# Retention followed by a convolution-gated unit: half of the convolution moved from TensorE to three other engines in every second unit

## The chip, the cores and the metric

The kernel runs on one core of one Trainium2 chip. The metric is the device time of one execution in microseconds (us), as the median of several. A core has five engines that matter here: TensorE (PE in the profile; PEld is its weight load), VectorE (DVE), ScalarE (ACT), GpSimd (POOL) and SyncE (SP), which only starts transfers. Each works through its own list of instructions in order and waits for the others through semaphores.

## What is computed

Two layers, one after the other. The first is a causal linear attention ("retention"), in which the score of two tokens decays with their distance. The second gates a projection of the result with the sigmoid of a causal convolution over five tokens, one weight per channel and tap.

```python
scores = scale * np.matmul(q, k.transpose(0, 1, 3, 2))       # (8, 8, 576, 576), head size 64
Dmat = np.where(rel >= 0, gamma[:, None, None] ** rel, 0.0)  # rel = row - column
x = np.matmul(scores * Dmat, v)                              # then heads joined: (8, 576, 512)
for k in range(5):
    gate_pre += conv_w[k] * xp[:, k:k + S, :]                # xp: x with four zero rows in front
gate = 1.0 / (1.0 + np.exp(-gate_pre))
out = (gate * (x @ w_val)) @ w_out                           # (8, 576, 512), float32
```

Products are taken in bfloat16 and summed in float32.

## The kernel before

**Tiles.** The 576 tokens of a batch are four whole chunks of 128 and a tail of 64; two tails of two batches share a chunk. That makes 36 chunks: four batches' whole chunks (0 to 15), their tails (16, 17), and the same for the other four batches (18 to 35). The first layer works chunk by chunk, the second on units of two chunks, so unit n is chunks 2n and 2n+1, and there are 18. In the second layer channels lie on partitions, in four blocks of 128.

**First layer, for a chunk t.** GpSimd starts the load of the keys (`load_keys`), scales and casts the values (`cast_v`) and casts the queries (`cast_q`). `turn_k` and `turn_q` transpose keys and queries on TensorE, four matmuls each, into a PSUM tile `tps`, of which there is one (`ps_t`, one buffer), and a copy takes it to SBUF: for keys on VectorE (kt), for queries on ScalarE (qtb, or qt for a tail). `scores` multiplies them into two PSUM banks, `masks(t, 0)` and `masks(t, 1)` apply the causal mask on VectorE (p). `carried` and `values` sum the chunk's output o from the running state and from p, and `take_x` scales it on VectorE into `xg`, which holds x for four batches with four zero columns ahead of each. `update` adds the chunk to the state in PSUM, `take_state` copies it out with two ScalarE instructions (sbd, or sbl at a batch's end).

**Second layer, for a unit n.** `conv` does the convolution as matmuls with diagonal weights `dg`: 64 x 64 tiles, four of which use different quarters of the array; five taps, four blocks, so 40 matmuls of 256 columns into two banks. In each half-block the order is such that a bank holds half of one block and half of another, and the value weights `wvb` and the output weights `wob` have their channels in the same mixed order. `gate` takes the sigmoid of a bank on ScalarE, `value` multiplies x with `wvb` (eight matmuls for each of two halves) and VectorE multiplies the gate into it (z). `project` multiplies z with `wob`, 128 tokens at a time, ScalarE copies the result (ob), SyncE stores it. The banks of conv, value and project come from one ring of three (`ps_g`).

**Order.** Nothing is planned by a scheduler: the program order is written out by hand, a head for chunks 0 to 3 and then a loop over t from 4 to 37, whose passes are called steps here. Step t does the state and output of chunk t, the scores of chunk t+1, `turn_k` of chunk t+2, the cast of v for t+2, the load of keys for t+4, and one or two `turn_q` for later batches (in steps 5 to 28, 32 and 33). An even step also does conv, gates and values of unit n = t/2 - 1, an odd step the projection of that unit:

```python
            n = t // 2 - 1
            ...
            if unit and not odd and n > 1:
                conv(n)
                gate(n, 0)
                gate(n, 1)
            if ok(t + 2) and t > 4:
                turn_k(t + 2)
            if ok(t) and odd:
                take_x(t)
            if ok(t + 1) and odd:
                masks(t + 1, 1)
            part = project if odd else value
```

So in an odd step VectorE's list is p, kt, x, p, and in an even one p, x, p, kt, z, z. In both, `turn_q` stands on TensorE between the two halves of `value` or `project`.

## Time and profile before

The median of three runs is 170.65 us (170.41 to 170.76). The profiled execution spans 169.9 us.

| what | us | instructions |
|---|---|---|
| conv's matmuls, line 385 | 23.2 busy | 720 |
| value's matmuls, line 400 | 36.9 busy | 288 |
| project's matmuls, line 411 | 36.5 busy | 144 |
| masks on VectorE, line 289 (128 x 512) | 0.686 each | 62 of the main form |
| take_x on VectorE, line 331 | 0.681 each | 31 |
| kt's copy on VectorE, line 249 | 0.423 each | 33 |
| gate on ScalarE, line 393 | 0.594 each | 36 |
| ob's copy on ScalarE, line 414 | 0.586 each | 36 |
| half of a state's copy on ScalarE, line 363 | 0.367 each | 64 |
| cast_v on GpSimd, line 221 | 1.049 each | 35 |
| start of a key load on GpSimd, line 96 | 0.941 each | 30 |

Busy time is the time in which an engine worked on at least one instruction of a group; matmuls overlap, so 720 of 271 ns give 23.2 us. A bracket at the end of a timeline line says how long the engine was idle before it and on whom it waited. The TensorE clock was granted in full over the whole span. 16 DMA engines moved 35.23 MB at 207 GB/s on average.

### The profile page before, as it was taken

The numbers are of one execution on the slowest core, as the hardware profiler recorded it, in microseconds if no ns is written. First come the engines' busy times: TensorE is split into PE (matmuls) and PEld (weight loads), VectorE is DVE, ScalarE is ACT, GpSimd is POOL, SyncE is SP. The second block draws the span as 40 slices with busy tenths as digits, with TensorE's granted clock in tenths as the row PEclk, the third lists the DMA queues.
The fourth block names the chain that finished last, engine by engine and source line by source line (L and its number), as shares of the span: only waits on it lengthen the run. The fifth ranks groups of instructions, "written<-read, shape, count | busy, mean of one in ns | idle before, by whom it ended". The sixth has DMA issues, their size and how long they took to land.

```text
span 169.9 us, 5543 instructions
## 1 busy us (share of the span) xinstructions
PE 154.0 (91%) x2297; PEld 110.4 (65%) x2297; DVE 114.3 (67%) x218; ACT 90.6 (53%) x184; POOL 97.9 (58%) x130
## 2 busy tenths in 40 slices
PE   6768874889999999999999999999999999999970
PEld 1344643645868686868677776868686867778630
DVE  6676670477676777777777768777777788786330
ACT  6754433736657556565437465755656543644330
POOL 8559999059279978487279338827986463000000
PEclk9999999999999999999999999999999999999999
DMA  4999999999999999999999999999999992303214
GB/s 124 291 198 275 319 198 270 193 185 169 287 296 275 252 235 221 129 237 280 272 198 171 281 258 183 202 289 276 253 267 190 190 230 92 124 3 127 83 44 123
DMA packets 93958, 35.23 MB, mean 207 GB/s; under 512 B 80090, under 2 KB 88814, under 8 KB 93934
## 3 DMA queue, kind: packets, MB, share of 16 engines
q1 hardware_dynamic: 57744, 29.63, 66.5%
q0 software_dynamic: 36000, 4.98, 43.0%
q8 instruction: 18, 0.29, 0.7%
q10 hardware_dynamic: 190, 0.27, 0.6%
q14 instruction: 6, 0.05, 0.1%
HBM read 30.42 MB, written 9.44 MB: 235 GB/s over the span
## 4 chain that ended last, share of the span: by engine, by line
PE 75%; DMA 9%; SPq 5%; DVE 3%; ACT 2%; issue 2%; POOL 1%; ACTq 0%; DVEq 0%
PE g L400 17%; PE g L411 16%; PE g L385 12%; PE tps L241 10%; PE s L280 6%; PE o L321 6%; DMA kb<-in_k_dram 5%; DMA fvc<-in_v_dram 4%; SPq L78 4%; PE st L352 3%; PE o L304 2%; SPq L119 1%; DVE p L289 1%; ACT ob L414 1%; ACT qtb L263 1%
## 5 line engine op out<-in xcount | busy, mean ns | idle before, releaser
L289 DVE TENSOR_TENSOR p<-s,maskq 128x512 bf16<-128x512 f32 x62 | 42.2, 686 | 16.6 <-PE s L280 16.4
L221 POOL TENSOR_TENSOR vb<-fvc,gin 128x512 bf16<-128x512 f32 x35 | 36.7, 1049 | 23.6 <-DMA fvc<-in_v_dram 7.5
L403 DVE TENSOR_TENSOR z<-gate,g 128x512 bf16<-128x512 f32 x36 | 24.8, 688 | 24.9 <-PE g L400 18.2
L400 PE MATMUL g<-xg,wvb 128*128 128x256 bf16 x288 | 36.9, 273 | 0.0
L411 PE MATMUL g<-wob,z 128*128 128x512 bf16 x144 | 36.5, 379 | 0.3 <-DVE z L403 0.3
L414 ACT COPY ob<-g 128x512 f32<-128x512 f32 x36 | 21.1, 586 | 27.7 <-PE g L411 27.4
L393 ACT ACTIVATE gate<-g 128x512 f32<-128x512 f32 x36 | 19.5, 594 | 20.8 <-PE g L385 20.8
L400 PEld LDWEIGHTS <-wvb 128*128 128x128 bf16 x288 | 26.5, 98 | 3.5 <-issue 0.8
L96 POOL DMA_DIRECT2D kb<-in_k_dram x30 | 28.2, 941 | 0.3 <-issue 0.2
L234 POOL CAST qb<-fqb 128x512 bf16<-128x512 f32 x27 | 16.6, 621 | 14.8 <-DMA fqb<-in_q_dram 14.8
L385 PE MATMUL g<-xg,dg 64*64 64x256 bf16 x720 | 23.2, 271 | 0.0
L363 ACT CAST sbd<-st 64x256 bf16<-64x256 f32 x48 | 17.6, 367 | 8.9 <-PE st L352 8.4
L331 DVE TENSOR_TENSOR xg<-o,gout 128x512 bf16<-128x512 f32 x31 | 21.1, 681 | 1.0 <-PE o L321 1.0
L385 PEld LDWEIGHTS <-dg 64*64 64x64 bf16 x720 | 18.4, 106 | 2.3 <-issue 0.8
L411 PEld LDWEIGHTS <-z 128*128 128x128 bf16 x144 | 12.5, 98 | 10.5 <-DVE z L403 1.2
L241 PE MATMUL tps<-ident,kb 128*128 128x128 bf16 x144 | 14.5, 224 | 2.6 <-DMA kb<-in_k_dram 1.7
L263 ACT COPY qtb<-tps 128x512 bf16<-128x512 bf16 x24 | 14.1, 589 | 4.2 <-PE tps L241 4.2
L280 PE MATMUL s<-qtb,kt 64*128 64x128 bf16 x248 | 12.3, 219 | 2.9 <-DVE kt L249 1.4
L249 DVE COPY kt<-tps 128x512 bf16<-128x512 bf16 x33 | 14.0, 423 | 0.9 <-PE tps L241 0.7
L321 PE MATMUL o<-p,vb 128*64 128x128 bf16 x280 | 14.5, 225 | 0.0
L241 PEld LDWEIGHTS <-qb 128*128 128x128 bf16 x144 | 10.9, 99 | 5.2 <-ACT qb L234 0.7
L241 PEld LDWEIGHTS <-kb 128*128 128x128 bf16 x144 | 8.5, 98 | 8.5 <-issue 2.8
(72 smaller groups left out, 147.0 us busy)
## 6 DMA issues: line engine op xcount, KB each, us to landing
fqb<-in_q_dram SPq DMA_DIRECT2D x8, 1024.0 KB, 9.2
fvc<-in_v_dram SPq DMA_DIRECT2D x32, 256.0 KB, 8.8
out_dram<-ob SPq DMA_DIRECT2D x32, 256.0 KB, 5.1
kb<-in_k_dram POOLq DMA_DIRECT2D x30, 128.0 KB, 8.4
wvf<-in_moe_w_val_dram SPq DMA_DIRECT2D x1, 1024.0 KB, 7.3
fqc<-in_q_dram SPq DMA_DIRECT2D x8, 128.0 KB, 5.9
fvc<-in_v_dram SPq DMA_DIRECT2D x8, 128.0 KB, 5.1
out_dram<-ob SPq DMA_DIRECT2D x6, 128.0 KB, 3.2
```

The lines of the kernel that those rows point to most:

```text
L96: nc.gpsimd.dma_start(out=kb, in_=k[b, :, c * P:(c + 1) * P, :].rearrange("h p d -> p h d"))
L221: eng.tensor_tensor(vb, loaded["v", *chunks[t]], gin[:, chunks[t][2], :].unsqueeze(2).to_broadcast([P, H, D]), op=ALU.mult)
L241: nc.tensor.transpose(ps[:, pr, :], flat[:, pr * P:(pr + 1) * P], ident)
L280: nc.tensor.matmul(s[i][:, pr, :], lhsT=kt[r, pr, :], rhs=queries(t, r, pr), start=(pr == 0), stop=(pr == NP - 1), skip_group_check=True)
L289: nc.vector.tensor_tensor(p, sps[t][i], m.unsqueeze(1).to_broadcast([P, NP, P]), op=ALU.mult)
L321: nc.tensor.matmul(o[r, pr, :], lhsT=vb[:, 2 * pr + i, :], rhs=pt[t, i][:, pr, :], start=(fresh and pr == 0), stop=(pr == NP - 1), skip_gr ...
L331: nc.vector.tensor_tensor(by_token(x[:, bl, :, PAD + i0:PAD + i0 + P]), ops[t].rearrange("p o (r n) -> p o n r", r=RQ), by_token(gout[:, : ...
L385: nc.tensor.matmul(g[bank][cols, pr, :], lhsT=dg[rows, blk, kk, :], rhs=xs(n, rows, blk, kk), start=(pr == 0 and kk == 0), stop=(pr == 1 a ...
L400: nc.tensor.matmul(vps[:, j, :], lhsT=wvb[:, o, 2 * i + j, :], rhs=xs(n, slice(0, P), o, PAD), start=(j == 0 and o == 0), stop=(j == 1 and ...
L403: nc.vector.tensor_tensor(z, gsb[n][i], vps, op=ALU.mult)
L411: nc.tensor.matmul(o, lhsT=zsb[n, j // 2][:, j % 2, i * P:(i + 1) * P], rhs=wob[:, j, :], start=(j == 0), stop=(j == NP - 1))
L414: nc.scalar.copy(ob, o)
```

## The change

In units 2, 4, ..., 16 (`aside`) the convolution of blocks 2 and 3 is no longer done by TensorE. Block 2 is summed on VectorE: one multiplication and four multiply-adds of 128 x 256 into a float32 tile `acc0`. Block 3 is done on ScalarE and GpSimd: ScalarE multiplies x by the tap's weight (an `Identity` activation with a scale per partition) and GpSimd adds the products into `acc1`. The sigmoid then takes two instructions a bank, one from PSUM and one from the sum in SBUF. As these blocks lie in natural order, such units use `wvn` and `won`, copies of the weights' second half in that order.

To give the taps time, everything of a unit comes one step later: conv, gates and values of unit n in step 2n+3 (in step 36 for the last), its projection in step 2n+4 (37 for the last). The taps are spread: the first one or two in step 2n+1, two more in 2n+2, the rest at the start of 2n+3. `take_x` and the second mask come ahead of `turn_k` in every step now. In the steps 2n+2 and 2n+3 of such a unit kt is copied on ScalarE instead of VectorE. Step 6 has no work of the second layer any more; step 36 has the projection of unit 16, and then conv and values of unit 17. The purpose is to take work off TensorE.

```diff
+        aside = set(range(2, NT // 2, 2))
+        def tap(eng, n, i, kk):
...
+            if i == 1:
+                t = a
+                if kk:
+                    t = gp.tile([P, 2 * P], F32, name="tap")
...
+                nc.scalar.activation(t, x, AF.Identity, scale=w)
+                if kk:
+                    nc.gpsimd.tensor_tensor(a, a, t, op=ALU.add)
+            elif kk == 0:
+                eng.tensor_scalar(a, x, w, None, op0=ALU.mult)
+            else:
+                eng.scalar_tensor_tensor(a, in0=x, scalar=w, in1=a, op0=ALU.mult, op1=ALU.add)
...
-            for pr in range(2):
+            for pr in range(1 if n in aside else 2):
...
+            if n in aside:
+                nc.scalar.activation(t[:, 0, :], gps[n][i][:, 0, :], AF.Sigmoid)
+                nc.scalar.activation(t[:, 1, :], acc[n, i], AF.Sigmoid)
...
+            first = next((n for n in range(2, NT // 2) if t == min(2 * n + 3, NT)), None)
+            second = 0 if t == 4 else 1 if t == 5 else next((n for n in range(2, NT // 2) if t == min(2 * n + 4, NT + 1)), None)
+            on_act = any(t in (2 * n + 2, 2 * n + 3) for n in aside)
...
+            for n in aside:
+                if t == 2 * n + 3:
+                    tap(None, n, 1, 4)
+                    tap(nc.vector, n, 0, 3)
+                    tap(nc.vector, n, 0, 4)
...
                 values(t)
-                if not odd:
-                    take_x(t)
-            if ok(t + 1) and not odd:
+                take_x(t)
+            if ok(t + 1):
                 masks(t + 1, 1)
-            if unit and not odd and n > 1:
-                conv(n)
-                gate(n, 0)
-                gate(n, 1)
+            if first is not None and t < NT:
+                conv(first)
+                gate(first, 0)
+                gate(first, 1)
             if ok(t + 2) and t > 4:
-                turn_k(t + 2)
-            if ok(t) and odd:
-                take_x(t)
-            if ok(t + 1) and odd:
-                masks(t + 1, 1)
+                turn_k(t + 2, s_copy if on_act else v_copy)
+            for n in aside:
+                if t == 2 * n + 1:
+                    tap(None, n, 1, 0)
+                    tap(None, n, 1, 1)
+                    tap(nc.vector, n, 0, 0)
+                if t == 2 * n + 2:
+                    tap(None, n, 1, 2)
+                    tap(None, n, 1, 3)
+                    tap(nc.vector, n, 0, 1)
+                    tap(nc.vector, n, 0, 2)
+            part, n = (value, first) if first is not None and t < NT else (project, second)
...
+            if t == NT:
+                conv(first)
+                for i in range(2):
+                    gate(first, i)
+                for i in range(2):
+                    value(first, i)
```

## The prediction

> **What bounds the kernel now.** I read the page's busy shares first, then its forty slices, then the costliest groups (the conv's, line 385, had no idle time before it), and last the timelines of two steps in the middle of the run, where the order on each engine can be seen. From the page:

> ```profile
> PE 154.0 (91%) x2297; PEld 110.4 (65%) x2297; DVE 114.3 (67%) x218; ACT 90.6 (53%) x184; POOL 97.9 (58%) x130
> ...
> PE   6768874889999999999999999999999999999970
> ```

> TensorE is the bound: from the tenth slice (about 40 us) to 160 us it is always at nine tenths or more, so an idle moment put into it there is added to the time, and work taken from it is won. The other figures of the first line leave room on every other engine, on average. Averages hide the order inside a step, so here are a conv step (from the scores at 106.54) and the project step after it (from 111.18). TensorE's timeline; L241 with kb is `turn_k`, with qb `turn_q`:

> ```profile
> 106.54 0.40 PE L280 MATMUL s<-qtb,kt 64*128 64x128 bf16 x8
> ...
> 107.21 1.29 PE L385 MATMUL g<-xg,dg 64*64 64x256 bf16 x40
> 108.43 0.40 PE L241 MATMUL tps<-ident,kb 128*128 128x128 bf16 x4
> ...
> 109.54 0.39 PE L241 MATMUL tps<-ident,qb 128*128 128x128 bf16 x4
> ...
> 111.18 0.40 PE L280 MATMUL s<-qtb,kt 64*128 64x128 bf16 x8
> ...
> 111.85 0.40 PE L241 MATMUL tps<-ident,kb 128*128 128x128 bf16 x4
> 112.08 1.03 PE L411 MATMUL g<-wob,z 128*128 128x512 bf16 x4
> 112.95 0.39 PE L241 MATMUL tps<-ident,qb 128*128 128x128 bf16 x4
> ```

> VectorE's timeline of the same steps, and two lines of ScalarE's:

> ```profile
> 106.97 0.69 DVE L289 TENSOR_TENSOR p<-s,maskq 128x512 bf16<-128x512 f32 x1 [0.70 <-PE s L280]
> 107.58 0.68 DVE L331 TENSOR_TENSOR xg<-o,gout 128x512 bf16<-128x512 f32 x1
> 108.17 0.68 DVE L289 TENSOR_TENSOR p<-s,maskq 128x512 bf16<-128x512 f32 x1
> 108.86 0.42 DVE L249 COPY kt<-tps 128x512 bf16<-128x512 bf16 x1
> ...
> 111.61 0.69 DVE L289 TENSOR_TENSOR p<-s,maskq 128x512 bf16<-128x512 f32 x1
> 112.28 0.42 DVE L249 COPY kt<-tps 128x512 bf16<-128x512 bf16 x1
> 112.63 0.68 DVE L331 TENSOR_TENSOR xg<-o,gout 128x512 bf16<-128x512 f32 x1
> ```

> ```profile
> 113.15 0.59 ACT L414 COPY ob<-g 128x512 f32<-128x512 f32 x1 [1.12 <-PE g L411]
> 113.63 0.59 ACT L263 COPY qtb<-tps 128x512 bf16<-128x512 bf16 x1
> ```

> What to see. The conv step lasts 111.18 - 106.54 = 4.64 us; the next scores come at 114.58, so the project step lasts 3.40. There is one `tps` bank: `turn_q` may write it only when the copy of kt has read it. In the project step VectorE copies kt second, ahead of `take_x`, and ends at 112.70; `turn_q` starts at 112.95, 1.77 after the step's start. In the conv step kt is copied fourth, after p, x and p, and ends at 109.28, which is 2.74 after the start. That is early enough there, because the conv holds `turn_q` back to 109.54, 3.00 after the start; in a project step it would be 1.0 us too late. On ScalarE a copy that has all it needs starts 0.48 after the one ahead of it (113.15 to 113.63), less than its 0.59.

> [...] two gates of 594 ns take 1.08 together, not 1.19. [...]

> **The change part by part.** A step is one pass of the loop.

> *Removed.* Half a conv in eight units. A whole one takes 108.43 - 107.21 = 1.22 us of TensorE, so 0.61 each: 7 x 0.61 = 4.3 in steps 7 to 33; the eighth is in the tail below. The natural-order weights `wvn` and `won` cost one DMA and two GpSimd casts (about 1.2 us, beside steps 5 and 6): nothing.

> *VectorE taps.* One tensor_scalar and four multiply-adds of 256 elements. [...] That makes 4 x 0.42 = 1.7 us in the aside's project step, 2n+2, which holds no z and, now, no kt copy: p, x, p end at about 2.5, taps at 4.1, or 0.7 into the next step. There they delay p, x and p by 0.3, which nobody feels. Contention could add up to one cast_v (1.05) to each tap; I take it as hidden and keep it for the range.

> *GpSimd adds.* Four of 256 elements, by half of cast_v's 1049 ns about 0.55 each: 2.2 per four steps, where 4 x 2.6 = 10.4 of 16.1 us are used. GpSimd now waits for ScalarE's taps instead of running ahead, so keys are asked for later: about two and a half steps, 9 to 10 us, before `turn_k`, against a median landing of 8.4 us (page, part 6). Mostly hidden; a few late ones belong to the range.

> *ScalarE.* [...] two gates become four of about 0.39, 0.31 apart; and kt is copied here in steps 2n+2 and 2n+3 (0.59, as for qtb). In order from the start of step 2n+2, with 0.48 from copy to copy: kt starts at 1.10 (when VectorE started it), taps at 1.58 and 1.98, ob 2.38, qtb 2.86, ob 3.34, the last tap 3.82, the state's two copies 4.22 to 4.97. That is 1.57 into step 2n+3. There come the four gates, to 2.81, and only behind them kt, to 3.40. TensorE reaches `turn_q` at 0.67 (scores, values) + 0.61 + 0.24 + 0.87 = 2.39 and waits for that copy: 1.07 us at full overlap. With no overlap the same sum ends at 4.4, a wait of 2.1. I take 1.2. Behind `turn_q` stand the second value, `carried` and `update`, the whole step. `turn_q` runs in steps 7, 11, 15, 19, 23, 27 of these (not 31 and 35): 6 x 1.2 = 7.2.

> *kt's place on VectorE.* take_x and the second mask now always come ahead of `turn_k`. In the project steps with kt on VectorE, 2n+4, the order is the conv step's: kt ends at 2.74, `turn_q` is due at 1.77. Wait 2.80 - 1.77 = 1.03, in steps 8, 12, 16, 20, 24, 28, 32: 7 x 1.03 = 7.2. In step 2n+1 the whole conv still covers it.

> *One step later.* Steps 7 to 33 now hold 14 conv steps and 13 project steps, against 13 and 14: 4.64 - 3.40 = +1.2. Step 6 loses conv and value, but what remains is a chain through one `tps` bank (state, kt, two taps, qtb, `turn_q`, qtb on ScalarE, about 4.4 us, against 5.15), and step 5's `turn_q` waits for kt after p, x, p (about +0.9): together step 7 starts about 0.2 later. In the tail, from the scores at 153.45 to the last conv at 159.60 were 6.15 us; now 0.33 + 0.34 + 1.73 (project 15) + 0.33 + 0.34 + 0.61 + 1.75 (value 16) + a wait of 0.49 for z + 1.73 (project 16) = 7.65: +1.5.

> Sum: -4.3 + 7.2 + 7.2 + 1.2 + 0.2 + 1.5 = +13.0, so 170.65 + 13.0 = 183.7 us.

> **The rivals.** (a) ScalarE keeps up. For it: its 53% share, and that all four steps together need some 13 us of it in 15.5. Against it: the excess falls in two neighbouring steps, where about 7 us of work is queued ahead of a copy with a deadline. Then 183.7 - 7.2 = 176.5. (b) More comes on top: VectorE's taps blocked by GpSimd until TensorE waits for take_x, or late keys. [...] against it: each first has to outlast the ScalarE wait. About 1 us for each of seven groups: 191. (c) TensorE stays the bound, the conv's 4.9 us are won and only the shift is paid: 170.65 - 4.3 + 1.2 + 0.2 + 1.5 = 169.3, faster. For it: the average shares; against it: both kt copies end after the moment at which `turn_q` is due by the trace's own distances. (d) Waits and savings cancel near 170.6.

> **How the numbers follow.** Forecast 0.62, (a) 0.16, (b) 0.15, (c) 0.05, (d) 0.02. The range 175.5 to 191.5 takes in (a) and the core of (b), and the forecast at a ScalarE wait of 2.1 us (6 x 0.9 more, 189). Faster 0.05, same 0.02, slower 0.93.

> **What would show it.** In the profile after: TensorE's row with eights in the middle; waits of tps (qb) for ACT kt and for DVE kt of about 1 us each, six and seven times; in step 2n+3, ScalarE never idle until kt; the conv group about 5 us less busy, 560 matmuls; a half conv of 0.6 us. I am wrong if those two waits are absent, if the waits of TensorE name kb's DMA or xg instead, or if the multiply-add is far over 0.42 us.

## The result, and the profile after

The changed kernel takes 199.65 us (median of four, 199.14 to 200.08), the kernel before on the same chip 170.7 (170.41 to 171.63): 1.164 times as long, interval 1.155 to 1.173. Ratios and intervals, here and below, leave out executions that the chip ran in a slower state, over 1.5% above the fastest of the same kernel. From the page of the kernel after:

```profile
span 198.0 us, 5308 instructions
...
PE 159.8 (81%) x2137; PEld 110.5 (56%) x2137; DVE 139.6 (71%) x244; ACT 114.7 (58%) x254; POOL 123.3 (62%) x165
...
PE   5868857877889879978992999298965999699990
...
PEclk9999999997899999999999699969996799999999
...
L405 DVE SCALAR_TENSOR_TENSOR acc<-xg,cw,acc 128x256 f32<-128x256 bf16 x32 | 32.2, 1005 | 0.9
...
L414 PE MATMUL g<-xg,dg 64*64 64x256 bf16 x560 | 19.4, 277 | 0.0
```

The conv's matmuls fell from 720 to 560, as meant, and from 23.2 to 19.4 us busy, 3.8 less where about 5 were forecast. But TensorE's row, a wall of nines before, has two 2s and later a 6, a 5 and a 6, and its clock row, full before, dips in the slice after each 2 and once more near the 5. A multiply-add (L405) takes 1005 ns on average; the 0.42 us of the prediction was its author's estimate (the kernel before took 415 ns for its own 128 x 256 operation with two input tensors, take_x of a tail, line 337). Who waits, from the waits view (us in total, times, longest):

```profile
PE tps L244 <- ACT kt L252: 15.5, 7, 3.9
...
ACT gate L424 <- DVE acc L405: 10.9, 7, 3.0
...
PE tps L244 <- DVE kt L252: 5.6, 6, 1.4
```

The two waits of TensorE that were forecast are there, but the one for ScalarE's kt is twice the size, and behind it stands a wait that was not in the sum: the sigmoid of the VectorE half waits for its multiply-adds. The conv step of unit 8 (step 19) shows how. TensorE's timeline:

```profile
101.21 0.40 PE L283 MATMUL s<-qtb,kt 64*128 64x128 bf16 x8
...
101.89 0.75 PE L414 MATMUL g<-xg,dg 64*64 64x256 bf16 x20
...
103.24 0.60 PE L434 MATMUL g<-xg,wvn 128*128 128x256 bf16 x4
107.72 0.38 PE L244 MATMUL tps<-ident,qb 128*128 128x128 bf16 x4 [3.88 <-ACT kt L252]
```

The step lasts 8.79 us, to the next scores at 110.01; such a step took 4.64 before. `turn_q` stands idle for 3.88 of it. VectorE, GpSimd and ScalarE at the same time:

```profile
99.55 0.68 DVE L292 TENSOR_TENSOR p<-s,maskq 128x512 bf16<-128x512 f32 x1
100.14 6.03 DVE L405 SCALAR_TENSOR_TENSOR acc<-xg,cw,acc 128x256 f32<-128x256 bf16 x4
```

```profile
99.96 0.61 POOL L237 CAST qb<-fqb 128x512 bf16<-128x512 f32 x1
100.53 1.60 POOL L401 TENSOR_TENSOR acc<-acc,tap 128x256 f32<-128x256 f32 x2
102.34 0.72 POOL L401 TENSOR_TENSOR acc<-acc,tap 128x256 f32<-128x256 f32 x1 [0.21 <-ACT tap L399]
103.01 0.94 POOL L96 DMA_DIRECT2D kb<-in_k_dram  x1
103.97 1.06 POOL L224 TENSOR_TENSOR vb<-fvc,gin 128x512 bf16<-128x512 f32 x1
104.96 0.61 POOL L237 CAST qb<-fqb 128x512 bf16<-128x512 f32 x1
```

```profile
102.84 0.38 ACT L423 ACTIVATE gate<-g 128x256 f32<-128x256 f32 x1
106.20 0.42 ACT L424 ACTIVATE gate<-acc 128x256 f32<-128x256 f32 x1 [2.98 <-DVE acc L405]
...
107.10 0.57 ACT L252 COPY kt<-tps 128x512 bf16<-128x512 bf16 x1
```

Four multiply-adds, 1.7 us by the estimate, hold VectorE for 6.03 us. GpSimd works almost without a pause meanwhile. Taken one by one, they end at 101.54, 102.41, 103.35 and 106.18, and the first three ends lie about 0.28 us after an add of GpSimd ended. The fourth, begun during a key load's start, outlives both casts that follow and takes 2.79. On ScalarE the gate of that sum waits 2.98 us, and kt's copy, which needs nothing of it, is queued behind. `turn_q` needs that copy, so the whole of TensorE's list stops.

All 32 multiply-adds, minimum, median and maximum in ns, from the view of tile acc:

```profile
L405 DVE SCALAR_TENSOR_TENSOR acc<-xg,cw,acc x32: 479/833/2791, 45.2 to 183.5; 128x256 f32<-128x256 bf16 x32
```

Nine of them, which met a GpSimd that was idle or just ending, or began before its next instruction, took 479 to 486 ns; the other 23 took 827 or more.

One more loss follows. The windows view (stretch, length, busy us of PE, PEld, DVE, ACT, POOL with instructions, granted clock, DMA share, GB/s):

```profile
105.19:108.60 3.41, 0.88 (x10) 0.80 (x10) 3.37 (x5) 1.93 (x5) 3.39 (x5) 1.00 1.50 152
108.60:112.01 3.41, 3.41 (x34) 2.43 (x32) 2.05 (x4) 0.86 (x3) 1.98 (x3) 0.50 0.72 46
```

By step lengths (from scores to scores): steps 4 to 33 take 26.8 us more than before, the tail (from the last scores on) 2.0 more, the head (all before step 4) 0.7 less; that is the 28.1 us between the two spans.

### The profile page after: what moved, and what is told of

It is laid out like the page before. It is cut to its first block, busy times and chain, and to the rows that moved or that the text cites. A ratio compares the mean times of both kernels' runs of the same rounds, so it can differ in the third digit from the quotient of the medians.

```text
span 198.0 us, 5308 instructions
## 1 busy us (share of the span) xinstructions
PE 159.8 (81%) x2137; PEld 110.5 (56%) x2137; DVE 139.6 (71%) x244; ACT 114.7 (58%) x254; POOL 123.3 (62%) x165
## 4 chain that ended last, share of the span: by engine, by line
DVE 36%; PE 28%; ACT 14%; DMA 8%; issue 4%; SPq 4%; POOL 3%; ACTq 0%; DVEq 0%; POOLq 0%
DVE acc L405 15%; DVE p L292 9%; PE g L434 6%; PE g L414 6%; PE g L446 5%; DVE z L437 5%; DMA kb<-in_k_dram 4%; DVE xg L334 4%; DMA fvc<-in_v_dram 4%; ACT gate L426 4%; PE tps L244 3%; SPq L78 3%; PE s L283 3%; ACT gate L424 2%; ACT kt L252 2%
## 5 line engine op out<-in xcount | busy, mean ns | idle before, releaser
L401 POOL TENSOR_TENSOR acc<-acc,tap 128x256 f32<-128x256 f32 x32 | 24.6, 768 | 46.8 <-ACT tap L399 45.9
L437 DVE TENSOR_TENSOR z<-gate,g 128x512 bf16<-128x512 f32 x36 | 24.5, 684 | 23.3 <-PE g L434 15.3
L446 PE MATMUL g<-wob,z 128*128 128x512 bf16 x112 | 33.1, 386 | 0.7 <-DVE z L437 0.7
L405 DVE SCALAR_TENSOR_TENSOR acc<-xg,cw,acc 128x256 f32<-128x256 bf16 x32 | 32.2, 1005 | 0.9
L434 PE MATMUL g<-xg,wvb 128*128 128x256 bf16 x224 | 31.3, 280 | 0.0
L244 PE MATMUL tps<-ident,qb 128*128 128x128 bf16 x124 | 12.1, 221 | 22.1 <-ACT kt L252 15.5
L434 PEld LDWEIGHTS <-wvb 128*128 128x128 bf16 x224 | 20.9, 100 | 3.1 <-issue 0.8
L414 PE MATMUL g<-xg,dg 64*64 64x256 bf16 x560 | 19.4, 277 | 0.0
L426 ACT ACTIVATE gate<-g 128x512 f32<-128x512 f32 x20 | 10.9, 595 | 13.2 <-PE g L414 13.2
L399 ACT ACTIVATE tap<-xg,cw 128x256 f32<-128x256 bf16 x32 | 15.6, 510 | 2.4 <-POOL acc L401 2.4
L414 PEld LDWEIGHTS <-dg 64*64 64x64 bf16 x560 | 14.3, 107 | 2.5 <-issue 1.0
```

The source lines that it names most:

```text
L244: nc.tensor.transpose(ps[:, pr, :], flat[:, pr * P:(pr + 1) * P], ident)
L401: nc.gpsimd.tensor_tensor(a, a, t, op=ALU.add)
L405: eng.scalar_tensor_tensor(a, in0=x, scalar=w, in1=a, op0=ALU.mult, op1=ALU.add)
L414: nc.tensor.matmul(g[bank][cols, pr, :], lhsT=dg[rows, blk, kk, :], rhs=xs(n, rows, blk, kk), start=(pr == 0 and kk == 0), stop=((pr == 1 ...
L434: nc.tensor.matmul(vps[:, j, :], lhsT=w, rhs=xs(n, slice(0, P), o, PAD), start=(j == 0 and o == 0), stop=(j == 1 and o == NP - 1), skip_gr ...
L437: nc.vector.tensor_tensor(z, gsb[n][i], vps, op=ALU.mult)
```

## The experiments

Each is compared with the kernel before on the same chip: 172.58 us for `one_input`, `kt_second`, `kt_before_gates` and `half_left_out`, 172.46 for `vector_memset`, `shift_only` and the two delays, 171.10 for the rest. The first eight were run once each, so their times have no interval; eleven executions of the kernel before on the last of these chips lie between 169.71 and 172.47, and a difference of 2 us in such a pair says little. What is inside their traces, wait by wait and step by step, carries the argument. An edit starts from the changed kernel unless it says otherwise.

### The multiply-add: held up by GpSimd, or only its form?

`one_input` has a multiplication in place of each multiply-add, so that only one operand comes from SBUF:

```diff
-                eng.scalar_tensor_tensor(a, in0=x, scalar=w, in1=a, op0=ALU.mult, op1=ALU.add)
+                eng.tensor_scalar(a, x, w, None, op0=ALU.mult)
```

> The changed kernel with the 32 multiply-adds of block 2 turned into multiplications (x times the tap's weight, written to the same tile): as many VectorE instructions at the same places with the same waits, but with one SBUF input instead of two. Left out: the summation of block 2. Blocking theory (an instruction with two SBUF inputs stands still while GpSimd works, and the second gate, kt and turn_q queue behind it): each falls from 1.0 us on average to 0.35 to 0.48, TensorE's seven waits for ScalarE's kt fall from 15.5 us together to about 7 x 0.8 = 6, no wait of TensorE is over 2 us, its clock stays at full speed but for one stretch near step 6, and the time falls by 9 for the waits and 7 for the clock, to about 183 to 185 us. ScalarE-queue theory (too much is queued on ScalarE ahead of kt, whatever VectorE does): the waits for kt stay at 12 us or more and the time above 195 us.

Measured: 188.35 us, against 199.65 for the changed kernel. The multiplications (a group of the page, and the view of tile acc) were not free of it either:

```profile
L405 DVE TENSOR_SCALAR acc<-xg,cw 128x256 f32<-128x256 bf16 x32 | 24.4, 763 | 0.8
```

```profile
L405 DVE TENSOR_SCALAR acc<-xg,cw x32: 343/754/2770, 43.7 to 171.9; 128x256 f32<-128x256 bf16 x32
```

The shortest took 343 ns, half of them 754 or more, and one took 2.77 us. TensorE still waited 9.3 us for ScalarE's kt, 3.7 of it behind that one. So the expectation that a multiplication is safe, because it reads one tensor from SBUF, fell. Both forms are lengthened in these places, the multiply-add by 0.53 us on average over its shortest (0.479 to 1.005), the multiplication by 0.42 (0.343 to 0.763).

`vector_memset` has a fill in the same place, which reads nothing:

```diff
-                eng.scalar_tensor_tensor(a, in0=x, scalar=w, in1=a, op0=ALU.mult, op1=ALU.add)
+                eng.memset(a, 0.0)
```

> The changed kernel with each multiply-add of block 2 replaced by a fill of the same tile with zeros, which reads nothing. Left out: the convolution of block 2 but for its first tap. Blocking theory: the 32 fills take about 0.35 us each whatever GpSimd does, the wait of the second gate for VectorE is gone, TensorE's seven waits for ScalarE's kt are about 0.7 to 1.1 us each (6 to 7.5 us together), as computed for ScalarE's queue alone, and the half-clock stretches in the middle of the run vanish; time 183 to 186 us. If waits of 2 us and more remain, something else than VectorE's reads holds ScalarE back.

Measured: 185.42 us. Its tile view, and a line of its waits:

```profile
L405 DVE MEMSET acc<- x32: 272/272/272, 47.4 to 168.8; 128x256 f32 x32
```

```profile
PE tps L244 <- ACT kt L252: 4.4, 6, 0.8
```

All 32 fills took the same 272 ns beside the same GpSimd work. The gate's wait for VectorE is gone, no wait for ScalarE's kt exceeds 0.8 us, and no stretch of half clock is left after 53 us. What is left is 185.42 - 172.46 = 13.0 us over the kernel before, as much as the prediction's whole sum, which had taken the multiply-adds as hidden. That the figures are equal is partly chance: TensorE waits 4.4 us for ScalarE's kt here, where 7.2 were forecast, and two stretches of half clock, from 28.98 and 49.46, were not forecast. The run is the cleanest evidence for the cause all the same: the fill keeps the position, the waits and the buffers and takes away only the reads and their time. It does not part these two: a fill is also shorter than a multiply-add that meets no GpSimd (0.27 against 0.48 us), but `one_input`, with a shortest time of 0.34, was still held up.

### The order of kt: which of the two waits binds, and what is behind it

`kt_second`: in the project steps in which VectorE copies kt, `turn_k` comes ahead of `take_x` again, as before the change.

```diff
+            early = not on_act and first is None and ok(t + 2) and t > 4
...
+                if early:
+                    turn_k(t + 2)
                 take_x(t)
...
-            if ok(t + 2) and t > 4:
+            if ok(t + 2) and t > 4 and not early:
```

> The changed kernel with turn_k ahead of take_x and of the second mask in those project steps in which VectorE copies kt, as before the change. Nothing left out. Order theory: TensorE's six waits for VectorE's kt (5.6 us together) vanish and nothing else moves: about 194 us. If these waits only take up slack that another wait would take in their place (the scores behind the second mask), the time stays within 1 us of 199.7.

Measured: 192.18 us. The waits for VectorE's kt are gone, those for ScalarE's stay:

```profile
PE tps L244 <- ACT kt L252: 14.9, 7, 3.9
```

The 7.5 us won against 199.65 are more than the 5.6 us of waits, though this compares one run with another chip's. By the traces, the project steps 8, 12, ..., 32 take 26.0 us together instead of 31.9. So 5.9 us of them were kt's place, a cost of its own, separate from the multiply-adds.

`kt_before_gates`: ScalarE's kt comes ahead of the gates.

```diff
                 conv(first)
-                gate(first, 0)
-                gate(first, 1)
             if ok(t + 2) and t > 4:
                 turn_k(t + 2, s_copy if on_act else v_copy)
+            if first is not None and t < NT:
+                gate(first, 0)
+                gate(first, 1)
```

> The changed kernel with turn_k emitted ahead of the two gates in the conv steps, so that ScalarE copies kt before it waits for the second half of the gate. Nothing left out. Blocking theory with the second gate as the only link: the seven waits of TensorE for kt vanish (15.5 us), and with them most half-clock stretches; what is left is that p, x and p stand behind the multiply-adds on VectorE, so that a new wait of about 1.5 us for take_x or for the gate's bank comes in the three worst steps; time 183 to 187 us. If the multiply-adds bound the step in any case, through p and take_x, the wait only changes its name and the time stays at 193 us or more. ScalarE-queue theory: kt moves ahead of four gates of 1.3 us, so each wait falls by 1.3 at most, 7 x 1.3 = 9 us in all: about 190 us.

Measured: 192.88 us. The waits for ScalarE's kt are gone from the steady state, but a new one has come, for take_x:

```profile
PE o L307 <- DVE xg L334: 7.3, 3, 2.5
```

take_x stands behind the blocked multiply-adds on VectorE itself, and these waits are 2.4 to 2.5 us each, not the 1.5 of the first expectation; the second, that the wait would only change its name, came closer, although 7 us were won. The order on ScalarE decided which product of the blocked VectorE was missed first, not whether one was.

`both_orders` makes both edits.

> The changed kernel with both orders mended: turn_k ahead of the gates in the conv steps, and ahead of take_x and the second mask in the project steps with kt on VectorE. Nothing left out. Blocking theory: the two gains add up as far as they are different waits (7 to 8 us each alone), but the multiply-adds still stand still behind GpSimd, so that about three waits of 2.5 us for take_x stay and with them half-clock stretches: 1.07 to 1.09 of the kernel before. If order were the whole cause: 0.98 of it.

Measured: 186.74 us (185.39 and 188.10), 1.0925 times before, interval 1.084 to 1.101. `turn_q`'s waits for kt shrink to 1.7 us in total, but the three waits for take_x, again 7.3 us, are untouched.

`all_three` adds the fill of `vector_memset` to them, so the multiply-adds and both orders, all that I blame, are mended together.

> Both orders mended, and each multiply-add replaced by a fill that reads nothing (left out: the convolution of block 2 but for its first tap). If blocking, ScalarE's queue, kt's place and the half clock that follows are the whole cause, what is left is the conv's 5.0 us won less the shift's 1.2 us: 0.975 to 0.985 of the kernel before, clock near 1.0 after the head. If something is still unaccounted for, 1.00 or more.

Measured: 173.28 us (172.76 and 173.81), 1.014 times before, interval 1.008 to 1.020. The loss is nearly gone, so the multiply-adds and the two orders make up most of it. On this one chip the changed kernel takes 200.71 us (`changed_again`, below), the orders take 14.0 off it (to 186.74) and the fill another 13.5: about half of the loss is order and half is the multiply-adds, and each half includes the half clock that followed. But the gain that I expected is not there, and by the expectation's own words something is still unaccounted for. From the start of step 10 to the start of step 34 the gain is there: 91.55 us against 94.08 in the kernel before, 2.5 less. Steps 5 to 9 cost 3.2 more, of which `shift_only` (below) has 1.3 too, and the tail 1.8. TensorE's timeline in those steps:

```profile
41.69 0.38 PE L244 MATMUL tps<-ident,qb 128*128 128x128 bf16 x4 [1.20 <-ACT qtb L266]
...
50.15 0.38 PE L244 MATMUL tps<-ident,qb 128*128 128x128 bf16 x4 [1.00 <-ACT kt L252]
...
58.18 0.40 PE L244 MATMUL tps<-ident,kb 128*128 128x128 bf16 x4 [1.20 <-DMA kb<-in_k_dram]
```

In step 5 a second query waits for ScalarE's copy of the first out of the one `tps` bank, which stands behind two taps and a copy of ob. In step 7 kt stands behind a tap that waited 1.87 us for an add of GpSimd, which had waited for queries to arrive. In step 9 a key load lands late.

### The saving and the shift by themselves

`half_left_out`, from the kernel before: the second half of the conv is dropped in units 2, 4, ..., 16, and its sigmoid reads a tile of zeros. Nothing is put on other engines and nothing shifts.

```diff
-            for pr in range(2):
+            for pr in range(1 if n in aside else 2):
...
+                nc.scalar.activation(t[:, 1, :], none, AF.Sigmoid)
```

> The kernel before the change with the conv of blocks 2 and 3 left out in units 2, 4, ..., 16, and their gate taken from a tile of zeros: no taps, no shift, the order as before. Left out: half of the convolution in eight units. It shows what the change could win at most. TensorE-bound theory: eight times 0.61 us, 170.7 - 4.9 = about 165.8 us. If a conv step is bound by VectorE or ScalarE as soon as TensorE is shorter, less than half of it: 168.5 us or more.

Measured: 167.61 against 172.58 us, 5.0 less. The steps say less: a conv step takes 4.34 us instead of 4.64, so 0.30 of the conv's 0.61 is won. The reason is the order seen in the prediction: there kt ends 2.74 us after the scores, and with half a conv `turn_q` is due at 2.39. In this run (the step from 104.20) kt ends 2.65 after the scores and `turn_q` starts 0.05 later. Against the profile of the kernel before, steps 4 to 33 save 2.4 us, the tail 0.5 and the head 1.1, where nothing was changed, 4.0 in all; the last 1.0 is that the kernel before was slower on this chip (a span of 170.8 us, mean clock 0.972) than where it was profiled (169.9, clock 1.000). So about 3 us of the 5.0 are the edit's. In `all_three`, where kt is not in the way, a halved conv step is 0.52 shorter.

`shift_only` is `kt_second` with no unit aside:

```diff
-        aside = set(range(2, NT // 2, 2))
+        aside = set()
```

> The changed kernel's order with no unit set aside: whole convs on TensorE, no taps, kt always on VectorE and, in project steps, ahead of take_x and the second mask as before the change. Nothing left out. It is the price of doing the second layer one step later. Predicted from the steps: +1.2 + 0.2 + 1.5, so 2.9 us over the kernel before; half-clock theory: 1.7 us more, for the light step 6, where TensorE also falls to half clock in the changed kernel. If the shift is free, the time is that of the kernel before within 0.5 us.

Measured: 173.68 against 172.46 us, 1.2 more where 2.9 were expected. Steps 4 to 33 cost 1.3, as computed, the tail 2.4, and the head, which the edit does not touch, happened to be 1.9 us shorter. There is no half clock in step 6. So the shift itself costs some 3.7 us, and eight halved conv steps at 0.52 win 4.2: by this estimate the change could gain next to nothing even without a wait. The 5.0 and 1.2 from which the expectation of `all_three` was made both contain such differences of the head.

### The lost clock

Both start from the kernel before and put fills of 912 ns on VectorE ahead of kt's copy, in five project steps; two or four of them:

```diff
+            if t in (9, 13, 17, 21, 25):
+                for _ in range(2):
+                    nc.vector.memset(idle, 0.0)
             if ok(t + 2) and t > 4:
                 turn_k(t + 2)
```

> The kernel before with two fills of an unused 128 x 1024 tile on VectorE ahead of kt's copy in steps 9, 13, 17, 21 and 25, so that TensorE waits at turn_q for about 2 us five times. Nothing left out. Additive theory (a wait costs its length): 5 x 2.0 = +10 us. Half-clock theory: short waits do not lower TensorE's clock, so the same +10 us with the clock at 1.0.

> The same with four fills: five waits of about 4.2 us. Additive theory: 5 x 4.2 = +21 us, clock at 1.0. Half-clock theory: each wait of about 4 us is followed by 3.4 us or more at half clock, which costs 1.7 us or more on top: +29 to +30 us, mean clock about 0.95.

Measured: 181.65 us with two and 203.35 with four, against 172.46. The waits:

```profile
PE tps L241 <- DVE kt L249: 9.0, 5, 1.9
```

```profile
PE tps L241 <- DVE kt L249: 21.0, 5, 4.3
```

With two fills, 9.0 us of waits cost 9.2, and the clock stays full. With four, 21.0 us of waits cost 30.9: after each of the five the clock is halved, for 6.83, 3.41, 6.83, 3.41 and 6.83 us. Here five waits of 4.2 us on average cost half as much again, and five of 1.8 cost about themselves. That a wait between these can bring it on too is seen in `kt_before_gates`, where the longest wait for take_x is 2.5 us; after a window in which TensorE was busy for 0.95 of 3.41 us, its clock was halved:

```profile
103.01:106.42 3.41, 0.95 (x11) 0.70 (x9) 3.41 (x4) 1.35 (x4) 3.39 (x5) 1.00 1.35 187
106.42:109.83 3.41, 3.19 (x30) 2.12 (x30) 3.41 (x7) 0.85 (x3) 3.02 (x4) 0.50 1.19 81
```

### Again, and a version that was to gain

`changed_again` is the changed kernel, on the same chip as `both_orders`, `all_three` and `late_two`.

> The changed kernel as it is, beside the others of this set. All theories: ratio to the kernel before 1.16 again.

Measured: 200.71 us (200.54 and 200.88), 1.174 times before, interval 1.168 to 1.181.

`late_two`, from the kernel before: no shift, only units 14 and 16 aside, in whose conv steps (30 and 34) there is no `turn_q`. VectorE's taps come after the second mask of step 2n+1, and the sigmoids of the two sums last of all gates. Excerpts of the edit:

```diff
+        aside = {14, 16}
...
+                for i in range(2):
+                    nc.scalar.activation(gsb[n][i][:, 1, :], acc[n, i], AF.Sigmoid)
...
+            nxt = n + 1 if odd and n + 1 in aside else None
+            if nxt:
+                for kk in range(KC):
+                    tap(nc.vector, nxt, 0, kk)
```

> The kernel before, in its own order, with units 14 and 16 alone set aside, where GpSimd has little left to do and no turn_q waits for kt; the taps stand behind the second mask of step 2n+1, two of ScalarE's behind the first half gate. Nothing left out. Blocking theory: with GpSimd mostly idle a multiply-add takes about 0.5 us, no wait of TensorE comes of it, and two half convs are won: 2 x 0.61 = 1.2 us, a ratio of 0.993. If VectorE's 2.3 us of taps in a 3.4 us step hold up masks or z, 1.00 or slower.

Measured: 173.92 to 177.70 us in six runs, 1.023 times before, interval 1.017 to 1.029, where 0.993 was forecast: a miss. Steps 30, 31 and 33 took 0.6, 1.6 and 1.4 us more than before. The multiply-adds took 658 ns on average, and in step 30 the last add of GpSimd came late, behind the starts of two key loads and a cast_v:

```profile
142.99 0.42 ACT L611 ACTIVATE gate<-acc 128x256 f32<-128x256 f32 x1 [2.43 <-POOL acc L400]
```

```profile
144.41 0.38 PE L444 MATMUL g<-won,z 128*128 128x512 bf16 x1 [1.39 <-DVE z L435]
```

That gate is followed by z on VectorE, and TensorE's projection waits for z. With two units only, the multiply-adds were held up less; here the chain began with GpSimd's own adds, of block 3. No version that computes the whole result was faster than the kernel before.

## Why the prediction was wrong

The direction was right, and so were the two orders through kt, `tps` and `turn_q`, which make up about half of the loss. The size was wrong: 29 us were lost where 13 were forecast.

**The step that failed.** "Contention could add up to one cast_v (1.05) to each tap; I take it as hidden". A multiply-add took 1005 ns on average, up to 2791, and it was not hidden: a fill in its place takes 13.5 us off the time (`both_orders` to `all_three`) or 14.2 (199.65 to `vector_memset`, on another chip), half clock included. So a term put at nothing was as large as the whole sum. A multiply-add far over 0.42 us was one of the prediction's own signs of being wrong. The working looked at VectorE's own list, where there was room, and not at who waits for the sum: the half gate, behind which kt is queued on ScalarE. So the term *ScalarE*, 6 x 1.2 = 7.2 us, became 14.8 us of waits in its six steps (and 0.72 in step 6): 0.74, 1.21 and 1.22 in the conv steps 7, 11 and 15, much as predicted, and 3.88, 3.86 and 3.86 in 19, 23 and 27, where a multiply-add of 2.8 us stood in front. The prices of two operations were too low even where nothing held them up: 0.48 us for a multiply-add that met no GpSimd, where 0.42 was estimated, and 0.72 for an add on GpSimd, where 0.55 was. With fills in place of the multiply-adds (`vector_memset`) no such wait exceeded 0.8 us. The spacing on ScalarE in that term, 0.40 us from tap to tap and 0.31 from half gate to half gate, was the author's estimate; the trace of the changed kernel has 0.42 (40.17 to 40.59) and 0.26 to 0.33 (in steps 7 and 19).

**What was missing.** The half clock. In steps 19, 23 and 27 the step grew by 4.12, 4.72 and 4.91 us over `shift_only` (8.79, 9.36 and 9.55 against 4.67, 4.64 and 4.64). Their waits are 3.88, 3.86 and 3.86, and half a conv saves some 0.5, so the slow stretches cost about 0.7, 1.4 and 1.6 us. The six conv steps with a `turn_q` together cost 44.5 us against 28.1 in `shift_only`, 16.4 more; predicted were 6 x (1.2 - 0.61) = 3.5. That is 12.9 of the 15.3 us by which steps 4 to 33 (26.8 measured, 11.5 predicted) were misjudged.

**What held.** *kt's place on VectorE*, 7.2 us: the seven project steps 8, 12, ..., 32 took 31.9 us against 24.2 in `shift_only`, 7.7 more. Of that 5.9 is kt's place, as `kt_second` shows; the rest includes stretches of half clock that reach into steps 20, 24 and 28, so that the sum comes so near to 7.2 is partly luck. *One step later* with the head's 0.2: 1.4 predicted for the steps, 1.3 measured in `shift_only`. The tail: 1.5 predicted, 2.0 measured, and 2.4 in `shift_only`. *Late keys*: none in the steps of the profile after; its one wait of TensorE for a key load, 1.4 us, lies in the head, where it was 1.7 before.

**What was too kind.** The saving of 0.61 us for each halved conv: 0.30 in the order of before and 0.52 in the best order tried.

**The rivals.** (b) had the mechanism: taps blocked by GpSimd until TensorE waits. It was sized at "about 1 us for each of seven groups", and named take_x as the one waited for; in the changed kernel kt's copy came first, and take_x only once kt was moved (`kt_before_gates`, `both_orders`). Behind the argument against it, "each first has to outlast the ScalarE wait", was a mistake: the two waits stand one behind the other on ScalarE, so they add up. (a) and (c) are refuted: ScalarE did not keep up, and even `all_three`, without these waits from step 10 on, was not faster.

## What to carry to other kernels

Before work is moved to VectorE beside a busy GpSimd, look at where its operands lie: here 23 of 32 multiply-adds, with all their operands in SBUF, lasted until a GpSimd instruction, or several, had ended (827 ns or more, against 479 to 486), while the masks, with one in PSUM, stayed at 0.68 us, and a free share of VectorE's time says nothing about that. Price a late result by what is queued behind its first reader, on that engine and then on the next; here a sigmoid held a copy that held all of TensorE. Half a conv of 0.61 us per step was bought with a chain over three engines that any one of them can break.

## What the runs showed of the hardware

**VectorE and GpSimd.** In the changed kernel a multiply-add took 479 to 486 ns where GpSimd was idle, just ending or began only after it, and 1005 on average. In `one_input` a multiplication in its place took 343 ns at the least and 763 on average; in `vector_memset` a fill, without inputs, always 272. VectorE's older operations, which take one input from PSUM, were not touched: the 62 masks took 675 to 692 ns in the changed kernel, 686 on average in the kernel before.

```profile
L292 DVE TENSOR_TENSOR p<-s,maskq 128x512 bf16<-128x512 f32 x62 | 42.1, 684 | 20.2 <-PE s L283 20.2
```

They read one tensor from SBUF too, so that alone does not lengthen an operation; why the multiplications were lengthened is not shown by these runs. The other side pays too: an add of GpSimd that began 0.06 us after a multiply-add took 1.01 us, where the median is 0.725. Whether the start of a key load holds up a multiply-add by itself stays open: one multiply-add ended 0.34 us into one, another that began 0.38 into one did not end in it.

**TensorE's clock.** In the clock records of the changed kernel and of `delay_4`, each of the stretches at half clock named above lasts 3.41 us or twice that; those of the changed kernel that begin at 108.60, 129.08 and 149.56 are 20.48 us apart, six times 3.413. The length of a gap did not decide. In `kt_before_gates` one of at most 2.5 us was enough; in the changed kernel a window whose longest gap is 0.89 us was followed by half clock; and in `delay_2` a window (56.89 to 60.30) with a gap of 1.79 us was not. The two lines are those of the changed kernel:

```profile
43.75:47.16 3.41, 1.57 (x22) 1.24 (x24) 3.30 (x7) 2.81 (x6) 1.64 (x2) 1.00 1.41 247
47.16:50.57 3.41, 3.41 (x44) 2.38 (x44) 2.00 (x4) 1.51 (x5) 2.72 (x5) 0.50 1.44 267
```

Divided into windows of 3.413 us that are aligned to the start of a slow stretch, the changed kernel has four at full clock, from 2.79 to 193.93 us, that were followed by half clock; in them TensorE was busy for 1.57, 0.88, 0.24 and 0.55 us, a share of 0.46 or less. In every other one at full clock it was busy for 2.02 us or more, a share of 0.59. The other runs, in the windows measured there: 0.95 us in `kt_before_gates` and 0.45 in `delay_4` were followed by half clock, 1.62 in `delay_2`, a share of 0.47, was not. So in these windows the busy share tells what follows better than the longest gap does: in the one from 43.75, two gaps of 0.72 and 0.89 us and a third of 0.23 came before a slow stretch, as one of 3.88 us did in step 19. What decides near a share of half is not shown.
